# Threshold attention into a gMLP block: new order of the gate branch, the weight preparation, the first clears and the last products

## The chip, the cores and the metric

One core of a Trainium2 chip runs the whole kernel. The metric is device time in microseconds (us), the median of several executions. The core's engines run side by side, each in its own program order: TensorE (PE; weight loads are listed as PEld), VectorE (DVE), ScalarE (ACT), GpSimd (POOL) and SyncE (SP). DMA transfers are issued from an engine's queue (SPq, POOLq, ACTq), also in order.

## The reference

```python
scores = scale * np.matmul(q, k.transpose(0, 1, 3, 2))          # 8 batches, 8 heads, 576 x 576
thresh = np.max(scores, axis=-1, keepdims=True) - tau
scores = np.where(scores >= thresh, scores, -1000000000.0)
attn = np.exp(scores - np.max(scores, axis=-1, keepdims=True))
attn = attn / (np.sum(attn, axis=-1, keepdims=True) + 1e-09)
x = (attn @ v), heads side by side                              # 8 x 576 x 512
h = np.maximum(x @ w_in, 0.0); u, v = halves of h               # 512 columns each
v_n = (v - mean) / np.sqrt(var + 1e-06)                         # over the 512 columns
v_s = np.einsum('ts,bsd->btd', w_spatial, v_n) + b_spatial[None, :, None]
out = (u * v_s) @ w_out                                         # float32
```

## The kernel before

Two heads make a pair; 32 pairs, four to a batch. A pair takes five **steps** (`g = 5 * slot + c`), one per block of 128 query rows (the fifth has 64). In a step TensorE forms the scores of both heads (L426, L429, into one of two `ps_s` buffers), VectorE takes the negated row maximum (`negm`, L472), ScalarE the exponential (`e`, L480), and one step later VectorE sets the values under the threshold to zero (`p`, L445; `pr`, L454, in the last block). SP then transposes the masked rows by DMA (`pT`, L449, once for two blocks; `ptr`, L457). So the 160 `negm` rows of VectorE mark the 160 steps; step 0 is the first.

Beside the scores each step carries up to two jobs, `f1` (before the maximum) and `f2` (at the step's end). In blocks 0 to 2 one of them prepares the next pair (transposes of q and k, L221 and L234); in blocks 3 and 4 one is `pv`, the product with v for the pair before (L261), whose result `xn` SP transposes into `xT` (L275). The other is a gMLP job of an earlier batch. There are 20 per batch:

- `moe_v` (five): half v of `x @ w_in` (L289), `vrel` on ScalarE (L314); one or two steps later a square with its sum (`sq`, L322), then a chain on GpSimd that ends in the normalised rows `vn` (L328).
- `moe_u` (five): half u, transposed (L340, L345).
- `moe_s` (five): the spatial product (L370, L375), each over all five `vn` blocks, and the gate `gT` on VectorE (L384).
- `moe_o` (five): the product with `w_out` (L399), a copy, a store (L410).

From step 27 on (`LAG`) batch b's jobs start at step 27 + 20b: v and u alternate over ten steps, then s and o alternate (o of the batch before). An `act` job used as `f2` is evaluated at the start of the next step (`held`). Each job takes one of two `ps_f` banks. The loads of q, k and v are popped from `queue`, one a step, ahead of the step's own work. A dictionary `chores` places the weight preparation: `w_in` at steps 5 to 11, `w_spatial` at 12 to 14, its casts and transposes at 16 to 20, the bias at 2 and 21, `w_out` at 23 and 25. After the last scores `last` lists the remaining jobs, two a step.

All clears of padding stand at the head of GpSimd's program. SP has one queue for loads, transposes and stores.

Of the kernel before, what the change touches and what calls it, by code (L numbers as in the profile page):

```python
# [17 lines left out]
def kernel(  # L18
# [49 lines left out]
    p_ring = [const.tile([P, 2, 1152], BF16, name=f"p{i}") for i in range(2)]
    pr_ring = [const.tile([P, 640], BF16, name=f"pr{i}") for i in range(2)]
# [4 lines left out]
    for ts in ld_ring:  # L74
        for t in ts:
            nc.gpsimd.memset(t[64:128, :, 4, :], 0.0)
    vx_ring = [const.tile([P, 2, D], F32, name=f"vx{i}") for i in range(2)]
    for t in vx_ring:
        nc.gpsimd.memset(t[0:64], 0.0)
    kd_ring = [const.tile([P, P], F32, name=f"kd{i}") for i in range(2)]  # L80
    for t in kd_ring:
        nc.gpsimd.memset(t, 0.0)
    for t in v_ring:
        nc.gpsimd.memset(t[:, :, D:D + 1], 1.0)
        nc.gpsimd.memset(t[64:128, 4, D:D + 1], 0.0)
        nc.gpsimd.memset(t[64:128, 9, D:D + 1], 0.0)
        nc.gpsimd.memset(t[0:64, 10, D:D + 1], 0.0)
    ptr_ring = [const.tile([P, 5, 192], BF16, name=f"ptr{i}") for i in range(3)]
    for t in ptr_ring:
        nc.gpsimd.memset(t[:, :, 128:192], 1.0)  # L90
    for t in pr_ring:
        nc.gpsimd.memset(t[:, S:640], 0.0)
    for t in vn_ring:
        nc.gpsimd.memset(t[64:128, 4, :], 1.0)

    w_in = const.tile([P, 4, 1024], BF16, name="w_in")
    w_o = const.tile([P, 4, 512], BF16, name="w_o")
# [1 line left out]
    wsb = const.tile([P, 5, 640], BF16, name="wsb")  # L99


    def load(i, n, w):

        b, hp = divmod(i, HP)
        t = ld_ring[i // 2 % 2][w][:, 2 * (i % 2):2 * (i % 2) + 2 * n]
        src = (q, k, v)[w][b, 2 * hp:2 * hp + 2 * n]

        def main():
            nc.sync.dma_start(
                out=t[:, :, 0:4, :],  # L110
                in_=src[:, 0:512, :].rearrange("h (p c) d -> p h (c d)", c=4))

        def rest():
            nc.sync.dma_start(out=t[0:64, :, 4, :],
                              in_=src[:, 512:576, :].rearrange("h p d -> p h d"))
# [130 lines left out]
    def pv(i, h):  # L246
        b, hp = divmod(i, HP)
        hold = {}
        vt = v_ring[i % 4]

        def mm():
            t = hold["t"] = bank()
            for c in range(5):
                for j in range(5):
                    if c < 4:
                        lhs = pts[i, c // 2][:, c % 2, 4 + (j + 1) % 5 if h else j, :]
                        rhs = vt[:, (10 if j == 4 else 5 + j) if h else j, :]
                    else:
                        lhs = pts[i, 2][:, j, 64 * h:64 * h + P]
                        rhs = vt[:, 5 * h + j, :]  # L260
                    nc.tensor.matmul(out=t[:, c * 65:c * 65 + 65], lhsT=lhs, rhs=rhs,  # L261
                                     start=(j == 0), stop=(j == 4))

        def ev():
            o = hold["t"][:, 0:325].rearrange("p (c d) -> p c d", d=65)
            if h == 0:
                xns[i] = xp.tile([P, 5, P], BF16, name="xn")
            r = small.tile([P, 5], F32, name="r")
            nc.vector.reciprocal(out=r, in_=o[:, :, 64])
            nc.vector.tensor_tensor(out=xns[i][:, :, h * D:(h + 1) * D], in0=o[:, :, 0:64],  # L270
                                    in1=r.unsqueeze(2).broadcast_to([P, 5, 64]), op=ALU.mult)
            if h == 1:
                if hp == 0:
                    xts[b] = xtp.tile([P, 4, 640], BF16, name="xT")
                nc.sync.dma_start_transpose(  # L275
                    out=xts[b][:, hp, :].rearrange("p (c s) -> p c s", s=P),
                    in_=xns[i].rearrange("p c d -> p (c d)"))
        return "dve", mm, ev

    us, gs = {}, {}  # L280
    later = []

    def moe_v(b, c):
        hold = {}

        def mm():
            t = hold["t"] = bank()
            for f in range(4):
# [103 lines left out]
    def moe_o(b, c):  # L392
        hold = {}
        n = P if c < 4 else 64

        def mm():
            t = hold["t"] = bank()
            for f in range(4):
                nc.tensor.matmul(out=t[:n], lhsT=gs[b][:, f, c * P:c * P + n],  # L399
                                 rhs=w_o[:, f, :], start=(f == 0), stop=(f == 3))  # L400

        def ev():
            o = orr.tile([P, 512], F32, name="o")
# [6 lines left out]
            nc.sync.dma_start(out=dst, in_=o[:n])  # L410
        return "act", mm, ev


# [45 lines left out]
    def step(i, c, f1, f2):  # L459

        if i is not None:
            s = scores(i, c)
# [14 lines left out]
        if i is not None:  # L477
            e = ep.tile([P, 2, S], F32, name="e")
            for h in range(nh):
                nc.scalar.activation(out=e[:, h, :], in_=s[:, h, :], func=ACT.Exp,  # L480
                                     bias=nm[:, h:h + 1])
        if unmasked:
            mask()
        if i is not None:
            unmasked.append((i, c, e))
        for f in due:
# [6 lines left out]
                held.append(f2[2])  # L493


    chores = {2: (load_bias, 0)}
    for n, g0, d, f in ((4, 5, 2, load_w_in), (3, 12, 1, load_ws), (5, 16, 1, shape_ws),
                        (1, 21, 1, shape_bias), (2, 23, 2, load_w_o)):
        chores.update({g0 + d * j: (f, j) for j in range(n)})

    LAG = 27
    jobs = {}
    for b in range(B - 1):
        for j in range(5):
            g = LAG + 20 * b + 2 * j
            jobs[g], jobs[g + 1] = (moe_v, b, j), (moe_u, b, j)
            jobs[g + 10] = (moe_s, b, j)
            if b:  # L510
                jobs[g + 11] = (moe_o, b - 1, j)
    last = [jobs.pop(g) for g in range(5 * NPAIR, LAG + 20 * B) if g in jobs]
    last += [(moe_o, B - 2, j) for j in range(5)]
    last[6:6] = [(pv, NPAIR - 1, h) for h in range(2)]
    last += [(f, B - 1, j) for f in (moe_v, moe_u, moe_s, moe_o) for j in range(5)]
    with tc.manual_schedule():
        for w in (0, 1):
            for f in load(0, 1, w):
                f()
        shape_qk(0)  # L520
        for f in (qk_main(0, 0), qk_main(0, 1), qk_rem(0)):
            f[1]()
            f[2]()
        for w in (0, 1):
            for f in load(1, 1, w):
                f()
        shape_qk(1)
        for f in load(0, 2, 2):
            f()
        queue = []  # L530
        for g in range(5 * NPAIR + (len(last) + 1) // 2):
            slot, c = divmod(g, 5)
# [64 lines left out]
```

## Time and profile before

| | us |
|---|---|
| median of 3 runs (581.0 to 581.65) | 581.09 |
| the profiled execution | 579.05 |
| its span, first to last instruction | 577.3 |
| mean granted TensorE clock | 0.94 |

The profile is of one execution; 1.75 us of its time lie outside the span. A row of a timeline has start, duration, engine, line, operation, tiles, and in brackets the idle time of the engine before it with what ended it. A count xN on a row means that neighbours were merged.

### The profile page before, as it was taken

What the parts mean: (1) busy time and instruction counts of PE and PEld (TensorE: products, weight loads), DVE (VectorE), ACT (ScalarE), POOL (GpSimd) and SP (SyncE); (2) the same over time, 40 slices, a digit from 0 to 9 for tenths busy, and PEclk for the clock granted to TensorE, in tenths of its full rate; (3) what the DMA queues carried; (4) which work ended last, traced back from release to release, by engine and by line L of the source; (5) the groups of instructions that cost most, each with busy time, mean ns of one, the idle gap of its engine ahead of it and who ended that gap; (6) DMA issues with size and microseconds to landing.
All of it is one profiled execution on the core that took longest, in us unless ns stands there. A gap on an engine that the chain in (4) does not pass through costs nothing.

```text
span 577.3 us, 10207 instructions
## 1 busy us (share of the span) xinstructions
PE 489.6 (85%) x3796; PEld 258.5 (45%) x3840; DVE 464.7 (81%) x512; ACT 329.3 (57%) x609; POOL 235.2 (41%) x436
## 2 busy tenths in 40 slices
PE   3785765996989699996999889996999969998896
PEld 2443333553545355553545445552555535553442
DVE  0897984995999779996999969995899959997543
ACT  1554451784557635784567835784557736685261
POOL 7532880275206612275206622276025722054010
PEclk9997985997999989998999989998999979998999
DMA  7599998978487876978698765977679677654732
GB/s 215 99 199 186 211 177 141 218 127 198 88 174 161 175 136 151 194 151 161 144 190 193 164 157 140 193 152 177 145 150 218 142 163 149 126 105 86 157 103 82
DMA packets 243601, 90.91 MB, mean 157 GB/s; under 512 B 213024, under 2 KB 238112, under 8 KB 243552
## 3 DMA queue, kind: packets, MB, share of 16 engines
q1 hardware_dynamic: 242352, 88.68, 73.9%
q0 software_dynamic: 1200, 1.58, 2.0%
q8 instruction: 30, 0.49, 0.3%
q14 instruction: 19, 0.16, 0.1%
HBM read 33.31 MB, written 9.44 MB: 74 GB/s over the span
## 4 chain that ended last, share of the span: by engine, by line
PE 47%; DVE 22%; issue 8%; POOL 7%; ACT 7%; DMA 7%; SPq 2%; POOLq 0%; ACTq 0%; DVEq 0%
PE s L426 18%; DVE negm L472 9%; DVE p L445 9%; PE f L261 7%; PE f L289 6%; PE s L429 4%; ACT e L480 3%; PE f L340 3%; PE f L370 3%; PE f L399 3%; DMA pT<-p 2%; PE f L221 2%; ACT sq L322 2%; DVE gT L384 1%; DMA ptr<-pr 1%
## 5 line engine op out<-in xcount | busy, mean ns | idle before, releaser
L480 ACT ACTIVATE e<-s,negm 128x576 f32<-128x576 f32 x288 | 199.6, 739 | 104.3 <-DVE negm L472 89.4
L472 DVE TENSOR_REDUCE negm<-s 128x2 f32<-128x1152 f32 (+1 forms) x160 | 197.1, 1232 | 45.8 <-PE s L426 44.3
L426 PE MATMUL s<-qkT 64*128 64x512 f32 (+1 forms) x768 | 194.3, 598 | 1.0 <-ACT e L480 1.0
L445 DVE SCALAR_TENSOR_TENSOR p<-e,ctau 128x1152 bf16<-128x1152 f32 x128 | 186.8, 1459 | 3.5 <-DMA pT<-p 3.5
L242 POOL COPY kd<-qkT 64x64 f32<-64x64 f32 x32 | 14.1, 442 | 168.2 <-ACT qkT L238 168.1
L261 PEld LDWEIGHTS <-pT 128*128 128x128 bf16 x1280 | 50.4, 101 | 43.9 <-issue 19.4
L426 PEld LDWEIGHTS s<-qkT 64*128 64x128 f32 (+1 forms) x768 | 56.7, 176 | 29.7 <-issue 3.7
L225 ACT COPY qkT<-f 128x512 f32<-128x512 f32 x64 | 37.6, 588 | 50.8 <-PE f L221 50.8
L429 PE MATMUL s<-kd,qkT 128*128 128x128 f32 x256 | 57.2, 307 | 10.9 <-ACT e L480 9.8
L261 PE MATMUL f<-v,pT 128*128 128x65 bf16 x1260 | 54.1, 199 | 14.2 <-DMA pT<-p 11.3
L370 PE MATMUL f<-wsT,vn 128*128 128x512 bf16 x130 | 38.5, 389 | 31.6 <-POOL vn L328 28.7
L429 PEld LDWEIGHTS s<-kd,qkT 128*128 128x128 f32 x256 | 46.3, 202 | 25.8 <-ACT e L480 11.5
L407 ACT COPY o<-f 128x512 f32<-128x512 f32 (+1 forms) x32 | 18.7, 583 | 53.8 <-PE f L399 51.8
L289 PE MATMUL f<-w_in,xT 128*128 128x512 bf16 x142 | 37.9, 380 | 5.5 <-ACT uT L355 5.1
L384 DVE TENSOR_TENSOR gT<-f,uT 128x512 bf16<-128x512 f32 x30 | 20.6, 686 | 25.9 <-PE f L370 22.2
L140 POOL COPY kn<-kl 128x640 f32<-128x640 f32 x32 | 31.1, 972 | 24.4 <-DMA kl<-in_k_dram 21.0
L370 PEld LDWEIGHTS <-vn 128*128 128x128 bf16 x160 | 14.8, 97 | 50.9 <-POOL vn L328 32.1
L316 POOL TENSOR_SCALAR nmean<-sm 128x1 f32<-128x1 f32 x35 | 15.7, 448 | 52.6 <-ACT vrel L314 52.6
L399 PE MATMUL f<-w_o,gT 128*128 128x512 bf16 (+1 forms) x126 | 36.5, 413 | 0.3 <-issue 0.2
L270 DVE TENSOR_TENSOR xn<-f,r 128x320 bf16<-128x320 f32 x63 | 31.0, 492 | 2.2
L328 POOL TENSOR_SCALAR vn<-vrel,rs,nm 128x512 bf16<-128x512 f32 (+1 forms) x35 | 30.4, 867 | 3.8
L340 PE MATMUL f<-xT,w_in 128*128 128x512 bf16 x104 | 29.9, 380 | 0.8
(92 smaller groups left out, 524.7 us busy)
## 6 DMA issues: line engine op xcount, KB each, us to landing
vl<-in_v_dram SPq DMA_DIRECT2D x16, 512.0 KB, 4.3
out_dram<-o SPq DMA_DIRECT2D x32, 256.0 KB, 2.5
ql<-in_q_dram SPq DMA_DIRECT2D x15, 512.0 KB, 4.3
kl<-in_k_dram SPq DMA_DIRECT2D x15, 512.0 KB, 5.1
uT<-in_moe_w_spatial_dram SPq DMA_DIRECT2D x2, 576.0 KB, 5.3
vl<-in_v_dram SPq DMA_DIRECT2D x16, 64.0 KB, 2.7
pT<-p SPq DMA_TRANSPOSE x64, 5.3
w_in<-in_moe_w_in_dram POOLq DMA_DIRECT2D x4, 256.0 KB, 5.6
```

The costliest lines, as they stand in the source:

```text
L140: nc.gpsimd.tensor_copy(out=t, in_=src)
L225: nc.scalar.copy(out=qks[i][:, which, 0:512], in_=hold["t"])
L261: nc.tensor.matmul(out=t[:, c * 65:c * 65 + 65], lhsT=lhs, rhs=rhs, start=(j == 0), stop=(j == 4))
L289: nc.tensor.matmul(out=t, lhsT=xts[b][:, f, c * P:(c + 1) * P], rhs=w_in[:, f, 512:1024], start=(f == 0), stop=(f == 3))
L340: nc.tensor.matmul(out=t, lhsT=w_in[:, m, f * P:(f + 1) * P], rhs=xts[b][:, m, 0:512], start=(m == 0), stop=(m == 3))
L370: nc.tensor.matmul(out=t, lhsT=vn[:, c, f * P:(f + 1) * P], rhs=wsT[:, c, 0:512], start=(c == 0), stop=(c == 4))
L399: nc.tensor.matmul(out=t[:n], lhsT=gs[b][:, f, c * P:c * P + n], rhs=w_o[:, f, :], start=(f == 0), stop=(f == 3))
L426: return nc.tensor.matmul(out=out, lhsT=qk[hs, 0, m], rhs=qk[hs, 1, lo:lo + n], start=True, stop=True)
L429: nc.tensor.matmul(out=view(s, 512, [[448, 2], [1, 64]]), lhsT=qk[:, 0, c * P:(c + 1) * P], rhs=kd_ring[i % 2], start=True, stop=True)
L445: nc.vector.scalar_tensor_tensor(out=pt[:, c % 2, :], in0=ef, scalar=ctau, in1=ef, op0=ALU.is_ge, op1=ALU.mult)
L472: nc.vector.tensor_reduce(out=nm[:, 0:nh], in_=s, axis=AX.X, op=ALU.max, negate=True)
L480: nc.scalar.activation(out=e[:, h, :], in_=s[:, h, :], func=ACT.Exp, bias=nm[:, h:h + 1])
```

## The change

It has six parts.

1. The order of a batch's jobs becomes `vuvvuvuvuu` then `oososososs`: all v by position 7, the first s at position 12 (it was 10, behind v at 8), the last at 19.
2. `chores` is spread: `w_in` at 6, 10, 14, 18; `w_spatial` at 8, 12, 16; the bias at 13, 15, and its three placing DMAs apart at 37; casts and transposes at 23, 26, 29, 32, 35; `w_out` at 42 and 47.
3. `sends`: the `xT` transposes and the stores are no longer issued where they arise but after the next mask, behind its `pT` or `ptr`.
4. The clears: three stay ahead of the first shaping; the others come behind pair 0's preparation, the bf16 ones on VectorE.
5. The first k load is issued from ScalarE's queue, the loads of pair 1 and v come earlier, and eight transposes of the identity run on TensorE first.
6. The tail: the last batch's v products run over the first three parts of the sum (`moe_v_part`) while the fourth `xT` is on its way, then over the fourth; the `moe_o` jobs of the batch before are dealt around them.

```diff
+    def clear_first():
+        for t in ld_ring[0][:2]:
             nc.gpsimd.memset(t[64:128, :, 4, :], 0.0)
+        nc.gpsimd.memset(kd_ring[0], 0.0)
+    def clear_rest():
+        ...
+        for t in ptr_ring:
+            nc.vector.memset(t[:, :, 128:192], 1.0)
...
-                nc.sync.dma_start_transpose(
+                xn = xns[i]
+                sends.append(lambda: nc.sync.dma_start_transpose(
...
+    def moe_v_part(b, c):
+        def mm():
+            if c % 3 == 0:
+                parted["tile"] = ps_s.tile([P, 1536], F32, name="s")
+            t = parted[c] = parted["tile"][:, 512 * (c % 3):512 * (c % 3) + 512]
+            for f in range(3):
+                nc.tensor.matmul(out=t, lhsT=xts[b][:, f, c * P:(c + 1) * P],
+                                 rhs=w_in[:, f, 512:1024], start=(f == 0), stop=False)
...
+        ready = sends[:]
+        sends.clear()
         if unmasked:
             mask()
+        for f in ready:
+            f()
...
-    chores = {2: (load_bias, 0)}
+    chores = {13: (load_bias, 0)}
...
+    ORDER = "vuvvuvuvuu" + "oososososs"
...
+    last += [(moe_o, Z - 1, j) for j in (0, 1)]
+    last += [(pv, NPAIR - 1, h) for h in range(2)]
+    last += [(moe_v_part, Z, j) for j in range(5)]
+    last += [(moe_v, Z, j) for j in range(5)]
+    last += [(moe_o, Z - 1, j) for j in (2, 3, 4)]
+    last += [(f, Z, j) for f in (moe_u, moe_s, moe_o) for j in range(5)]
...
-            for f in load(0, 1, w):
+            for f in load(0, 1, w, (nc.sync, nc.scalar)[w]):
                 f()
+        clear_first()
...
+        for _ in range(8):
+            nc.tensor.transpose(out=ps_f.tile([P, 512], F32, name="f")[:, 0:P], in_=identf,
+                                identity=identf)
```

TensorE before, behind batch 1's last u product (L345, step 56): scores (L429, L426), the remainder's transposes (L234), then the first spatial product.

```order
L345 LDWEIGHTS w_in
L345 MATMUL f<-xT,w_in 128x64
L429 MATMUL s<-kd_135,qkT 128x2x64
L426 MATMUL s<-qkT 128x512 x2
L234 MATMUL f<-identf,qn 128x128
L234 MATMUL f<-identf,kn 128x128
L370 LDWEIGHTS vn_117
L370 MATMUL f<-wsT,vn_117 128x512
```

The same place of the changed kernel, whose lines have other numbers (L364 is the last u product, L418 the product with `w_out`).

```order
L364 LDWEIGHTS w_in
L364 MATMUL f<-xT,w_in 128x64
L448 MATMUL s<-kd_120,qkT 128x2x64
L445 MATMUL s<-qkT 128x512 x2
L239 MATMUL f<-identf,qn 128x128
L239 MATMUL f<-identf,kn 128x128
L418 LDWEIGHTS gT
L418 MATMUL f<-w_o,gT 128x512
```

Where the spatial product stood there is now a product of the batch before; the spatial one follows two steps later.

SP's queue before, around the fourth `xT` of a batch (steps 63 to 65; `ql_118` is the next load of q).

```order
L449 DMA_TRANSPOSE pT<-p_108 128x18x128
L410 DMA out_dram<-o 128x512 x2
L449 DMA_TRANSPOSE pT<-p_109 128x18x128
L275 DMA_TRANSPOSE xT<-xn 128x5x128
L109 DMA ql_118<-in_q_dram 128x4x256
L457 DMA_TRANSPOSE ptr_154<-pr_110 128x5x128
L114 DMA ql_118<-in_q_dram 64x4x64
```

The same stretch of the changed kernel (L281 is `xT`, L476 is `ptr`, L429 a store).

```order
L468 DMA_TRANSPOSE pT<-p_101 128x18x128
L429 DMA out_dram<-o 128x512
L468 DMA_TRANSPOSE pT<-p_102 128x18x128
L429 DMA out_dram<-o 64x512
L111 DMA ql_111<-in_q_dram 128x4x256
L476 DMA_TRANSPOSE ptr_121<-pr_103 128x5x128
L281 DMA_TRANSPOSE xT<-xn 128x5x128
```

The fourth `xT` has moved behind the load of q and behind `ptr`.

GpSimd before, at the first shaping (`qn`, `kn`); 28 more clears and the identity stand ahead of these rows.

```order
L90 MEMSET ptr_156 128x5x64
L92 MEMSET pr_110 128x64
L92 MEMSET pr_111 128x64
L94 MEMSET vn_116 64x512
L94 MEMSET vn_117 64x512
L137 TENSOR_SCALAR qn<-ql_118 128x640
L140 COPY kn<-kl_119 128x640
```

The changed kernel's GpSimd from its first clear on.

```order
L76 MEMSET ql_111 64x4x64
L76 MEMSET kl_112 64x4x64
L77 MEMSET kd_119 128x128
masks.py:197 MEMSET identf 128x128
masks.py:199 ISA
masks.py:199 AFFINE_SELECT identf<-identf 128x128
L139 TENSOR_SCALAR qn<-ql_111 128x640
L142 COPY kn<-kl_112 128x640
```

Three clears and the identity are left ahead of `qn`.

## Rows read from the trace of the kernel before

**Rows 1.** The page's busy time by engine.

```profile
PE 489.6 (85%) x3796; PEld 258.5 (45%) x3840; DVE 464.7 (81%) x512; ACT 329.3 (57%) x609; POOL 235.2 (41%) x436
```

**Rows 2.** Who waited for whom: total us, times, longest.

```profile
PE f L370 <- POOL vn L328: 28.7, 7, 4.4
```

**Rows 3.** Timeline of TensorE around batch 2's first spatial product.

```profile
263.34 1.02 PE L370 MATMUL f<-wsT,vn 128*128 128x512 bf16 x3
...
268.75 0.39 PE L370 MATMUL f<-wsT,vn 128*128 128x512 bf16 x1 [4.38 <-POOL vn L328]
...
269.36 2.08 PE L426 MATMUL s<-qkT 64*128 64x512 f32 x4
...
277.02 1.13 PE L426 MATMUL s<-qkT 64*128 64x512 f32 x4
```

**Rows 4.** Timeline of ScalarE and GpSimd in the same stretch.

```profile
265.76 0.72 ACT L322 ACTIVATE sq<-vrel,nmean 128x512 bf16<-128x512 f32 x1
...
267.93 0.76 POOL L328 TENSOR_SCALAR vn<-vrel,rs,nm 64x512 bf16<-64x512 f32 x1
```

**Rows 5.** Timeline of VectorE: maxima of steps 0, 11, 26, 72, 74, 77, 78, 79, 98.

```profile
14.44 1.36 DVE L472 TENSOR_REDUCE negm<-s 128x2 f32<-128x1152 f32 x1 [13.55 <-PE s L426]
...
43.71 1.35 DVE L472 TENSOR_REDUCE negm<-s 128x2 f32<-128x1152 f32 x1
...
101.33 1.35 DVE L472 TENSOR_REDUCE negm<-s 128x2 f32<-128x1152 f32 x1
...
248.82 1.36 DVE L472 TENSOR_REDUCE negm<-s 128x2 f32<-128x1152 f32 x1 [0.94 <-PE s L426]
...
254.66 0.75 DVE L472 TENSOR_REDUCE negm<-s 128x1 f32<-128x576 f32 x1
...
263.06 1.34 DVE L472 TENSOR_REDUCE negm<-s 128x2 f32<-128x1152 f32 x1
...
271.49 1.36 DVE L472 TENSOR_REDUCE negm<-s 128x2 f32<-128x1152 f32 x1 [1.62 <-PE s L426]
...
274.95 0.76 DVE L472 TENSOR_REDUCE negm<-s 128x1 f32<-128x576 f32 x1
...
337.37 1.36 DVE L472 TENSOR_REDUCE negm<-s 128x2 f32<-128x1152 f32 x1 [1.75 <-PE s L426]
```

**Rows 6.** Stretches of 10 us: busy PE, PEld, DVE, ACT, POOL, clock, DMA, GB/s.

```profile
40.00:50.00 10.00, 6.82 (x40) 3.20 (x38) 6.87 (x7) 4.76 (x8) 1.44 (x1) 1.00 1.27 154
...
300.00:310.00 10.00, 9.89 (x91) 5.63 (x93) 9.70 (x12) 6.88 (x14) 3.02 (x8) 1.00 0.91 222
```

**Rows 7.** Timeline of SP's queue and TensorE at batch 3's first v product.

```profile
296.12 1.24 SPq L275 DMA_TRANSPOSE xT<-xn  x1
...
298.30 1.57 SPq L457 DMA_TRANSPOSE ptr<-pr  x1
...
299.60 1.23 PE L289 MATMUL f<-w_in,xT 128*128 128x512 bf16 x3
```

**Rows 8.** DMA issues: count, KB each, median us from issue to landing.

```profile
kl<-in_k_dram SPq DMA_DIRECT2D x2, 32.0 KB, 3.1
...
xT<-xn SPq DMA_TRANSPOSE x32, 2.6
```

**Rows 9.** Timeline of the first 13 us.

```profile
2.67 0.63 SPq L114 DMA_DIRECT2D kl<-in_k_dram  x1
...
7.39 0.73 POOL L137 TENSOR_SCALAR qn<-ql 128x640 f32<-128x640 f32 x1
...
12.31 2.08 PE L426 MATMUL s<-qkT 64*128 64x512 f32 x4
```

**Rows 10.** Timeline of TensorE before step 24.

```profile
90.37 0.73 PE L261 MATMUL f<-v,pT 128*128 128x65 bf16 x10 [7.22 <-DMA pT<-p]
```

**Rows 11.** Timeline of the tail: the last transpose and the first v product.

```profile
547.27 1.21 SPq L275 DMA_TRANSPOSE xT<-xn  x1
...
553.17 1.04 PE L289 MATMUL s<-w_in,xT 128*128 128x512 bf16 x4
```

More of the change, by code (lines that the diff above doesn't have):

```diff
@@ L73 @@
                for i in range(2)]
-    for ts in ld_ring:
-        for t in ts:
-            nc.gpsimd.memset(t[64:128, :, 4, :], 0.0)
[L77 to L94, printed above, removed]
+    vx_ring = [const.tile([P, 2, D], F32, name=f"vx{i}") for i in range(2)]
+    kd_ring = [const.tile([P, P], F32, name=f"kd{i}") for i in range(2)]
+    ptr_ring = [const.tile([P, 5, 192], BF16, name=f"ptr{i}") for i in range(3)]
+    def clear_first():
+        for t in ld_ring[0][:2]:
+            nc.gpsimd.memset(t[64:128, :, 4, :], 0.0)
+        nc.gpsimd.memset(kd_ring[0], 0.0)
+    def clear_rest():
+        nc.gpsimd.memset(ld_ring[0][2][64:128, :, 4, :], 0.0)
+        nc.gpsimd.memset(kd_ring[1], 0.0)
+        for t in vx_ring:
+            nc.gpsimd.memset(t[0:64], 0.0)
+        for t in ld_ring[1]:
+            nc.gpsimd.memset(t[64:128, :, 4, :], 0.0)
+        for t in v_ring:
+            nc.vector.memset(t[:, :, D:D + 1], 1.0)
+            nc.vector.memset(t[64:128, 4, D:D + 1], 0.0)
+            nc.vector.memset(t[64:128, 9, D:D + 1], 0.0)
+            nc.vector.memset(t[0:64, 10, D:D + 1], 0.0)
+        for t in ptr_ring:
+            nc.vector.memset(t[:, :, 128:192], 1.0)
+        for t in pr_ring:
+            nc.vector.memset(t[:, S:640], 0.0)
+        for t in vn_ring:
+            nc.vector.memset(t[64:128, 4, :], 1.0)
     w_in = const.tile([P, 4, 1024], BF16, name="w_in")
@@ L99, with load @@
     wsb = const.tile([P, 5, 640], BF16, name="wsb")
-    def load(i, n, w):
+    def load(i, n, w, eng=nc.sync):
         b, hp = divmod(i, HP)
@@ L108, in main @@
         def main():
-            nc.sync.dma_start(
+            eng.dma_start(
                 out=t[:, :, 0:4, :],
@@ L113, in rest @@
         def rest():
-            nc.sync.dma_start(out=t[0:64, :, 4, :],
-                              in_=src[:, 512:576, :].rearrange("h p d -> p h d"))
+            eng.dma_start(out=t[0:64, :, 4, :],
+                          in_=src[:, 512:576, :].rearrange("h p d -> p h d"))
         def rest_b():
@@ L196, in shape_bias, with place_bias @@
         nc.gpsimd.tensor_copy(out=parts[:, 2, :], in_=b32)
+    def place_bias(_):
         for n in range(3):
@@ L210 @@
     done_with = set()
+    sends = []
     qks, pts, xns, xts = {}, {}, {}, {}
@@ L274, in ev @@
                     xts[b] = xtp.tile([P, 4, 640], BF16, name="xT")
-                nc.sync.dma_start_transpose(
+                xn = xns[i]
+                sends.append(lambda: nc.sync.dma_start_transpose(
                     out=xts[b][:, hp, :].rearrange("p (c s) -> p c s", s=P),
-                    in_=xns[i].rearrange("p c d -> p (c d)"))
+                    in_=xn.rearrange("p c d -> p (c d)")))
         return "dve", mm, ev
@@ L281 @@
     later = []
+    parted = {}
+    def moe_v_part(b, c):
[6 more added lines that the diff above has]
+                                 rhs=w_in[:, f, 512:1024], start=(f == 0), stop=False)
+        return "act", mm, lambda: None
     def moe_v(b, c):
@@ L286, in mm @@
         def mm():
-            t = hold["t"] = bank()
-            for f in range(4):
+            t = hold["t"] = parted.get(c) if b == B - 1 else bank()
+            for f in range(3 if b == B - 1 else 0, 4):
                 nc.tensor.matmul(out=t, lhsT=xts[b][:, f, c * P:(c + 1) * P],
@@ L409, in ev @@
                    else out[b, 512:576, :])
-            nc.sync.dma_start(out=dst, in_=o[:n])
+            sends.append(lambda: nc.sync.dma_start(out=dst, in_=o[:n]))
         return "act", mm, ev
@@ L493, in step @@
                 held.append(f2[2])
-    chores = {2: (load_bias, 0)}
-    for n, g0, d, f in ((4, 5, 2, load_w_in), (3, 12, 1, load_ws), (5, 16, 1, shape_ws),
-                        (1, 21, 1, shape_bias), (2, 23, 2, load_w_o)):
+    chores = {13: (load_bias, 0)}
+    for n, g0, d, f in ((4, 6, 4, load_w_in), (3, 8, 4, load_ws), (5, 23, 3, shape_ws),
+                        (1, 15, 1, shape_bias), (1, 37, 1, place_bias), (2, 42, 5, load_w_o)):
         chores.update({g0 + d * j: (f, j) for j in range(n)})
@@ L503 @@
     LAG = 27
+    ORDER = "vuvvuvuvuu" + "oososososs"
     jobs = {}
     for b in range(B - 1):
[L506 to L511, printed above, removed]
-    last = [jobs.pop(g) for g in range(5 * NPAIR, LAG + 20 * B) if g in jobs]
-    last += [(moe_o, B - 2, j) for j in range(5)]
-    last[6:6] = [(pv, NPAIR - 1, h) for h in range(2)]
@@ L515 @@
-    last += [(f, B - 1, j) for f in (moe_v, moe_u, moe_s, moe_o) for j in range(5)]
+        n = dict.fromkeys("vuso", 0)
+        for j, t in enumerate(ORDER):
+            f = {"v": moe_v, "u": moe_u, "s": moe_s, "o": moe_o}[t]
+            if t != "o" or b:
+                jobs[LAG + 20 * b + j] = (f, b - (t == "o"), n[t])
+            n[t] += 1
+    last = [jobs.pop(g) for g in range(5 * NPAIR, LAG + 20 * B) if g in jobs]
+    Z = B - 1
+    last += [(moe_o, Z - 1, j) for j in (0, 1)]
+    last += [(pv, NPAIR - 1, h) for h in range(2)]
@@ L516 @@
+    last += [(moe_v_part, Z, j) for j in range(5)]
+    last += [(moe_v, Z, j) for j in range(5)]
+    last += [(moe_o, Z - 1, j) for j in (2, 3, 4)]
+    last += [(f, Z, j) for f in (moe_u, moe_s, moe_o) for j in range(5)]
     with tc.manual_schedule():
         for w in (0, 1):
-            for f in load(0, 1, w):
+            for f in load(0, 1, w, (nc.sync, nc.scalar)[w]):
                 f()
+        clear_first()
+        make_identity(nc, identf)
+        nc.vector.memset(ntau, -float(tau))
+        nc.vector.memset(mhalf, -0.5)
+        nc.scalar.activation(out=ctau, in_=ntau, func=ACT.Exp)
+        for w in (0, 1):
+            for f in load(1, 1, w):
+                f()
+        for f in load(0, 2, 2):
+            f()
+        for _ in range(8):
+            nc.tensor.transpose(out=ps_f.tile([P, 512], F32, name="f")[:, 0:P], in_=identf,
+                                identity=identf)
@@ L523 @@
             f[2]()
-        for w in (0, 1):
-            for f in load(1, 1, w):
-                f()
+        clear_rest()
         shape_qk(1)
-        for f in load(0, 2, 2):
-            f()
         queue = []
@@ L561 @@
             held.pop(0)()
+        for f in sends:
+            f()
 _INS = ['q', 'k', 'v', 'tau', 'moe_w_in', 'moe_w_spatial', 'moe_b_spatial', 'moe_w_out']
```

4 lines of the change are left out of this document (removed).

## The prediction

> **What bounds the kernel now.** I read the page's busy times first. TensorE is busy for 85% of the span, VectorE for 81% [rows 1]: both near full, so an average names no bound and the stages have to be read apart. The maxima of VectorE give the stages, one row a step [rows 5]. Steps 0 to 11 take 43.71 - 14.44 = 29.27 us, 2.66 us a step, with no gMLP jobs in them. Steps 11 to 26 take 101.33 - 43.71 = 57.6 us, where fifteen such steps would take 39.9: 17.7 us too much. From step 27 on the pattern repeats every 20 steps; steps 78 to 98 take 337.37 - 271.49 = 65.9 us. In such a stretch 10 us without a stall show TensorE busy for 9.89 and VectorE for 9.70 [rows 6], so what is left to gain there is the stalls.
>
> The list of waits names the stall: TensorE waits for `vn` seven times, 28.7 us in all [rows 2], once per batch that has scores beside it. The timeline shows one: three of the five matmuls of the first spatial product run at 263.34, the last starts at 268.75 behind an idle of 4.38 us, and the scores behind it take 2.08 us for four where they take 1.13 later [rows 3]. TensorE thus ran at about half its later speed after the wait, its 1.2 GHz level against 2.4, though only the row's duration shows that so sharply. What it waited for is the last block's square on ScalarE at 265.76 and the GpSimd chain that ends with `vn` at 267.93 [rows 4]. The fifth v product stands two steps ahead of the first spatial product and its square one step later, in the same step in which TensorE already stands at the product.
>
> **The change part by part.** *Job order (the main term).* The step pair with the stall, 77 and 78, takes 274.95 - 263.06 = 11.89 us. The pair 72 and 73 holds the same blocks (2 and 3) with two ordinary jobs and takes 254.66 - 248.82 = 5.84 us [rows 5]. One stall so costs 6.05 us: 4.38 of waiting and 1.67 of slow matmuls. Scaled to all seven waits that is 28.7 x 6.05 / 4.38 = 39.6 us. In the changed order the last v is at position 7 and in block 4, where its `vrel` is taken in the same step; its square falls into position 8, and the spatial product stands at 12. Three to four steps of about 3 us lie between, against a chain of 268.75 - 265.76 = 3 us. The wait goes, and no matmul is added: the same 20 jobs stand in the 20 steps. Bounds: at least the bare 28.7 us if the slow matmuls were hidden by VectorE anyway, at most 43 us (six pairs like this one and the last batch). I take 39.6, since the step difference is measured whole. What is late next is TensorE itself: 65.9 - 6.05 = 59.8 us for 20 steps of which it is busy nearly throughout.
>
> *The later `xT`.* A new wait: SP now issues the fourth `xT` of a batch behind the load of q and behind `ptr`. In the rows `xT` was issued at 296.12 and lands a median 2.6 us after issue, at 298.7, and the first v product began at 299.60, 0.9 us later [rows 7, 8]. The fourth matmul, which needs that part, comes some 0.65 us behind the first (three of 1.23 us, overlapping). With the two instructions exchanged, `ptr` goes out at about 297.0 and `xT` behind its 1.57 us, at 298.6, landing at 301.2; TensorE wants it at 300.3. That is 0.9 us, less the bit by which the wait before it fills; I take 0.8 us x 7 batches = 5.6 us lost. Behind the waiting product stand the next step's scores, for which VectorE then waits. Bounds: nothing, if the steps ahead are longer; 7 x (0.9 + 1.67) = 18 us, if each wait also costs a slow stretch like the one above. Its nearest rows are waits under 1 us, so I stay near the lower part. The stores deferred with it cost nothing: they are behind `pT` instead of ahead, and three `o` buffers cover them.
>
> *Chores.* Steps 11 to 26 lose 17.7 us. DMA is more than full at 40 to 50 us (busy share 1.27) [rows 6], and before step 24 TensorE waits 7.22 us for a `pT` [rows 10] that stands in SP's queue behind transposes of the spatial weights, which wait for GpSimd's casts. The change takes four of five of those transposes, the placing of the bias and both loads of `w_out` out of these steps, and starts two of four `w_in` loads later. All `w_in` and `w_spatial` bytes still fall within steps 6 to 18. I leave 5 us of the 17.7, so 13 gained; bounds 3 (only the later half of one stall) and 17.7. What was moved to steps 27 to 47 lies beside jobs on a TensorE that is nearly full, and GpSimd, at 41%, has room; I charge 1 us, from 0 to 5. The loads of `w_out` are due at step 57, the bias at 39; neither is near.
>
> *Start.* `qn` starts at 7.39, when GpSimd's list of clears ends; the last k load was issued at 2.67 and lands a median 3.1 us later, at 5.8 [rows 8, 9]. Three clears and the identity end well before that. With k issued beside q, from about 1.3, everything lands by 4.4 to 5, and step 0 starts 2.5 to 3 us earlier. The clears moved behind it (about 2 us on GpSimd) lie where TensorE makes pair 0's scores; the ones on VectorE lie in the 13.55 us it waits [rows 5]. I take 3.4 us with the second pair's loads, which no longer wait behind pair 0; bounds 0.5 (only DMA order) and 6. The eight extra transposes end before the data are there and I cost them at nothing. The first scores run slow at 12.31 (2.08 us) although ten transposes had run just ahead [rows 9]. The Trainium skill (TensorE: Matmul & The Clock Gate, Part 4: PE-mode transpose) says that transposes do not count as busy for the clock; by that the eight gain nothing, otherwise the sum would be about 2 us lower. The Trainium skill (DMA: Bandwidth & Descriptors, Issuing engines are not separate DMA queues) says that issuing from a second engine saves only the time to initiate; by that the k load gains no more than the issue rows of q, and the start term would be nearer 2.
>
> *Tail.* The last `xT` is issued at 547.27, lands at about 549.9, and the v products start at 553.17 behind six jobs put there to fill the wait [rows 8, 11]. In the new order 15 of the 20 v matmuls fill it and only five follow. Part of them still runs slow after the wait for `ptr`, so I place the first complete v product at 551.6, some 2.6 us before its old end, 554.2. From there VectorE sets the pace, five statistics and five normalisations, and it keeps the lead. `ptr` is issued 0.6 us later, since `xT` goes ahead of it. Gain 2.0; bounds -1 (a loss) and 5.
>
> **The sum**, against the profiled 579.05 us: -39.6 + 5.6 - 13 + 1 - 3.4 - 2.0 = -51.4, which gives 527.65. The median of the runs lies 2.04 above the profiled execution, so 529.7 us.
>
> **Rivals.**
> - *The start stays bound by DMA.* For: all w_in and w_spatial traffic still falls into steps 6 to 18, at a share already over 1 [rows 6]. Against: the 7.22 us wait comes of the weight transposes, which are moved. Then 3 instead of 13: 540 us. Chance 0.17.
> - *`xT` and TensorE take more back.* TensorE is the bound between the stalls [rows 6], and a late `xT` hits it there. With 2 us a batch instead of 0.8 the time is 538. Chance 0.13.
> - *The stall only moves: the change doesn't do what it says.* GpSimd works in order, and casts of weights or loads awaited ahead of the `vn` chain could keep `vn` last for position 12. Half the main term lost: 549.5. Against it: four steps of margin to a 3 us chain. Chance 0.05.
> - *Slower: the SP queue becomes the bound.* Without the stall SP has 60 us instead of 66 for the same DMAs, and the fourth `xT` stands at the end of its queue. If it landed 7.6 us after issue (5 more than the median) in all seven batches, each wait would be 0.8 + 5 + 1.67 = 7.5 us, 52 instead of 5.6, and if the same crowding kept the 13 us of the chores, the time is 529.7 + 46.7 + 13 = 589. It decides from a wait of some 6.3 us per batch on. Against: only a few `xT` are late now; the v products wait for one hardly at all [rows 7]. Chance 0.05, of which 0.01 within the bound of no change.
> - *All parts work in full:* no late `xT`, all 17.7 us of the chores back, 3 us more at both ends: 516. Chance 0.08.
>
> **How the numbers follow.** The forecast, 529.7, has 0.52, with a range of its own of 520 to 538. To hold 8 in 10 the range takes in the case above it (540), the low bounds of the start and tail, and much of the 538 case with both together: 516 to 546. Left out are the moved stall, the slower case and the best case's lower half, about 0.14. A difference under 0.2% (1.2 us) could not be told from none. Faster 0.95, same 0.01, slower 0.04.
>
> **What would show it.** In the changed profile the wait of the spatial product for `vn` should be gone, the step with position 10 should take about 2.8 us and 20 steps about 60.5; the v product should wait for `xT` under 1 us per batch; step 0's maximum should stand at 11, step 26's near 85; the last v should end near 553. The forecast is wrong if 20 steps still take over 62 us, or step 26 comes after 95.

## The result and the profile after

The changed kernel takes 564.6 us (median; 562.84 to 566.71) against 581.05 before: ratio 0.973, 95% interval 0.968 to 0.978. It is faster, but 35 us slower than forecast and outside the range. The profiled execution took 562.84 us, its span is 561.1. Ratios here and below are of executions in the chip's usual state; in the run "xT at once" two of four were in a slower one, the profiled one among them.

The busy time by engine answers to [rows 1]: TensorE does the same work in a shorter span.

```profile
PE 487.0 (87%) x3848; PEld 257.7 (46%) x3848; DVE 470.5 (84%) x535; ACT 328.2 (59%) x609; POOL 240.8 (43%) x413
```

In the list of waits of the changed kernel (total us, times, longest) nothing stands for `vn` and the spatial product any more: the row of [rows 2] is gone. The waits of `pv` for `ptr` have grown (6.0 us in four waits before). New are those of the v product (L308) for `xT`, and two for a bank that ScalarE still reads (`vrel`). The wait for `uT` is now one of the u product (it was 5.1 us, of the v product).

```profile
PE f L266 <- DMA ptr<-pr: 19.2, 10, 6.1
...
PE f L308 <- DMA xT<-xn: 9.5, 5, 3.4
...
PE f L359 <- ACT vrel L333: 5.8, 7, 0.8
...
PE f L266 <- ACT vrel L333: 4.6, 7, 0.7
PE f L364 <- ACT uT L374: 4.5, 6, 0.8
```

The maxima of VectorE (L491 now) at steps 0, 11, 26, 57, 77, 97, 157 and 159 answer to [rows 5].

```profile
12.47 1.36 DVE L491 TENSOR_REDUCE negm<-s 128x2 f32<-128x1152 f32 x1 [8.13 <-PE s L445]
...
41.67 1.35 DVE L491 TENSOR_REDUCE negm<-s 128x2 f32<-128x1152 f32 x1
...
93.81 1.35 DVE L491 TENSOR_REDUCE negm<-s 128x2 f32<-128x1152 f32 x1
...
193.22 1.36 DVE L491 TENSOR_REDUCE negm<-s 128x2 f32<-128x1152 f32 x1 [0.63 <-PE s L445]
...
256.27 1.36 DVE L491 TENSOR_REDUCE negm<-s 128x2 f32<-128x1152 f32 x1 [0.63 <-PE s L445]
...
323.31 1.36 DVE L491 TENSOR_REDUCE negm<-s 128x2 f32<-128x1152 f32 x1 [0.63 <-PE s L445]
...
512.67 1.34 DVE L491 TENSOR_REDUCE negm<-s 128x2 f32<-128x1152 f32 x1
...
518.64 0.75 DVE L491 TENSOR_REDUCE negm<-s 128x1 f32<-128x576 f32 x1
```

Steps 57 to 77 take 256.27 - 193.22 = 63.1 us, 77 to 97 67.0, where 60.5 was forecast and more than 62 was to show the forecast wrong. The differences of such rows give the stages, with the best experiment on the cause (nothing deferred, below) in the last column:

| profiled span, us | before | changed | nothing deferred |
|---|---|---|---|
| to step 0 | 14.4 | 12.5 | 12.3 |
| steps 0 to 11 | 29.3 | 29.2 | 29.6 |
| steps 11 to 26 | 57.6 | 52.1 | 47.4 |
| steps 26 to 57 | 95.3 | 99.4 | 99.7 |
| steps 57 to 157 | 329.0 | 319.5 | 303.7 |
| steps 157 to 159 | 9.3 | 6.0 | 6.0 |
| behind step 159 | 42.4 | 42.5 | 39.3 |

How a batch's first v product goes in the changed kernel answers to [rows 7]. First SP's queue: the load of q, `ptr`, then the fourth `xT`.

```profile
284.69 0.55 SPq L111 DMA_DIRECT2D ql<-in_q_dram  x1
285.34 1.24 SPq L476 DMA_TRANSPOSE ptr<-pr  x1
286.63 2.85 SPq L281 DMA_TRANSPOSE xT<-xn  x1
```

Then TensorE: three of four matmuls, 3.36 us of idle, the fourth, and scores that take 1.61 us instead of 1.13.

```profile
288.03 0.81 PE L308 MATMUL f<-w_in,xT 128*128 128x512 bf16 x3 [0.22 <-DVE gT L406]
292.19 0.39 PE L308 MATMUL f<-w_in,xT 128*128 128x512 bf16 x1 [3.36 <-DMA xT<-xn]
...
292.73 1.61 PE L445 MATMUL s<-qkT 64*128 64x512 f32 x4
```

The granted clock was 1.00 from 280 to 288 us; behind the wait it was 0.61, for the most part the lower of TensorE's two levels (1.2 GHz; full speed is 2.4). In the answer below it is the third number from the end, ahead of the DMA share.

```profile
292.50:296.00 3.50, 3.50 (x12) 1.03 (x11) 1.62 (x2) 0.69 (x2) 0.19 (x1) 0.61 1.11 284
```

From issue to the matmul are 292.19 - 286.63 = 5.6 us; [rows 8] had a median of 2.6 for the landing. Four of the five transposes that TensorE waited for stood behind a load of q that was still under way; they landed 3.6 to 5.5 us after issue. Over all `xT` of the changed kernel (minimum, median, maximum):

```profile
DMA to landing us min/median/max: 2.6/3.4/5.5
```

### The profile page after: what moved, and what is told of

It is laid out like the page before. It is cut to its first block, busy times and chain, and to the rows that moved or that the text cites. A ratio compares the mean times of both kernels' runs of the same rounds, so it can differ in the third digit from the quotient of the medians.

```text
span 561.1 us, 10240 instructions
## 1 busy us (share of the span) xinstructions
PE 487.0 (87%) x3848; PEld 257.7 (46%) x3848; DVE 470.5 (84%) x535; ACT 328.2 (59%) x609; POOL 240.8 (43%) x413
## 4 chain that ended last, share of the span: by engine, by line
PE 47%; DVE 24%; DMA 12%; ACT 10%; issue 5%; SPq 1%; POOL 0%; ACTq 0%; POOLq 0%
PE s L445 18%; DVE negm L491 14%; PE f L266 7%; DVE p L464 7%; DMA ptr<-pr 7%; ACT e L499 5%; PE f L389 4%; DMA xT<-xn 4%; PE s L448 3%; PE f L359 3%; PE f L308 3%; PE f L418 3%; ACT sq L341 2%; DVE xn L275 1%; ACT vrel L333 1%
## 5 line engine op out<-in xcount | busy, mean ns | idle before, releaser
L491 DVE TENSOR_REDUCE negm<-s 128x2 f32<-128x1152 f32 (+1 forms) x160 | 197.2, 1233 | 47.3 <-PE s L445 45.9
L445 PE MATMUL s<-qkT 64*128 64x512 f32 (+1 forms) x768 | 191.1, 590 | 1.0 <-ACT e L499 1.0
L445 PEld LDWEIGHTS s<-qkT 64*128 64x128 f32 (+1 forms) x768 | 55.6, 173 | 29.2 <-issue 2.8
L448 PE MATMUL s<-kd,qkT 128*128 128x128 f32 x256 | 55.4, 299 | 8.5 <-ACT e L499 5.5
L308 PE MATMUL f<-w_in,xT 128*128 128x512 bf16 x140 | 37.8, 387 | 11.0 <-DMA xT<-xn 9.5
L142 POOL COPY kn<-kl 128x640 f32<-128x640 f32 x32 | 26.1, 817 | 32.8 <-DMA kl<-in_k_dram 20.3
L335 POOL TENSOR_SCALAR nmean<-sm 128x1 f32<-128x1 f32 x35 | 11.8, 338 | 64.8 <-ACT vrel L333 64.8
L266 PE MATMUL f<-v,ptr 128*128 128x65 bf16 x315 | 21.2, 199 | 19.2 <-DMA ptr<-pr 19.2
L359 PE MATMUL f<-xT,w_in 128*128 128x512 bf16 x120 | 32.6, 396 | 5.8 <-ACT vrel L333 5.8
L139 POOL TENSOR_SCALAR qn<-ql 128x640 f32<-128x640 f32 x32 | 30.5, 953 | 11.6 <-DMA ql<-in_q_dram 10.7
L418 PE MATMUL f<-w_o,gT 128*128 128x512 bf16 (+1 forms) x128 | 33.8, 388 | 0.5
L333 ACT ACTIVATE vrel<-f 128x512 f32<-128x512 f32 x35 | 20.8, 595 | 20.8 <-PE f L308 20.8
L473 DVE SCALAR_TENSOR_TENSOR pr<-e,ctau 128x576 bf16<-128x576 f32 x32 | 31.9, 997 | 0.0
```

Of the source, the lines that this page charges most:

```text
L359: nc.tensor.matmul(out=t, lhsT=w_in[:, m, f * P:(f + 1) * P], rhs=xts[b][:, m, 0:512], start=(m == 0), stop=(m == 3))
L445: return nc.tensor.matmul(out=out, lhsT=qk[hs, 0, m], rhs=qk[hs, 1, lo:lo + n], start=True, stop=True)
L448: nc.tensor.matmul(out=view(s, 512, [[448, 2], [1, 64]]), lhsT=qk[:, 0, c * P:(c + 1) * P], rhs=kd_ring[i % 2], start=True, stop=True)
L491: nc.vector.tensor_reduce(out=nm[:, 0:nh], in_=s, axis=AX.X, op=ALU.max, negate=True)
```

## The experiments

Each run is compared with the kernel before, run on the same chip in the same call; ratios carry their 95% interval. The changed kernel's is 0.973.

**xT at once.** The deferral is undone for `xT` alone:

```diff
-                sends.append(lambda: nc.sync.dma_start_transpose(
+                nc.sync.dma_start_transpose(
```

> The changed kernel, but xT is issued on SP where xn arises, as before; the stores stay deferred. Theory Q (order in SP's queue): the fourth xT of a batch lands late because it stands behind the 512-KB load of q and ptr; issued first, the five waits of TensorE for it (9.5 us) and the slow matmuls behind them (some 2 us) go: about 553 where the changed kernel has 564.6. Rival D (the DMA engines are full once the vn stall is gone): what xT gains ptr and pT lose, within 2 us of 564.6.

Ratio 0.936 (0.928 to 0.944). The rival is out: `ptr` loses nothing that `xT` gains (TensorE's waits for it are 12.9 us, against 19.2 in the changed kernel). More came back than the 11 us expected.

**Only the job order**, in the kernel before:

```diff
+    ORDER = "vuvvuvuvuu" + "oososososs"
...
-            jobs[g], jobs[g + 1] = (moe_v, b, j), (moe_u, b, j)
-            jobs[g + 10] = (moe_s, b, j)
...
+                jobs[LAG + 20 * b + j] = (f, b - (t == "o"), n[t])
```

> The kernel before with the new job order alone (xT and stores at once, weight preparation, clears and tail as before). Theory Q: the vn stall goes and nothing is put behind loads, so the whole main term shows: 581 - 40 = 541, 20 steps in about 60 us. Rival D: without the stall the transposes land late all the same, 20 steps take 63 to 65 us as in the changed kernel: 560 to 568.

548.2 us, ratio 0.945 (0.939 to 0.950). So the order alone is worth 580.3 - 548.2 = 32.1 us, more than all six parts together, and the rival (20 steps in 63 to 65 us) is out: they take 60.9, as the maxima of steps 57 and 77 show.

```profile
194.12 1.36 DVE L472 TENSOR_REDUCE negm<-s 128x2 f32<-128x1152 f32 x1 [0.63 <-PE s L426]
...
255.05 1.36 DVE L472 TENSOR_REDUCE negm<-s 128x2 f32<-128x1152 f32 x1 [0.63 <-PE s L426]
```

**The old job order** in the changed kernel:

```diff
-    ORDER = "vuvvuvuvuu" + "oososososs"
+    ORDER = "vuvuvuvuvu" + "sososososo"
```

> The changed kernel with the job order of before; all else changed. Theory Q: the seven waits for vn come back (about 40 us with slow matmuls), and in their slack the waits for xT (9.5 us plus 2) go: 564.6 + 40 - 11 = about 593. Rival D (the transposes had always needed that time, the stall only hid it): the stall costs what the lateness costs, 564 to 572.

592.4 us, ratio 1.020 (1.013 to 1.027): the other parts of the change, without the order, make the kernel slower. The maxima of steps 77 and 97 in this run are 69.4 us apart, 3.9 more than before the change. The stall for `vn` does not hide the late transposes as Theory Q had it: both waits stand in the list, and both are paid, though the total came out as that theory said.

```profile
263.04 1.34 DVE L491 TENSOR_REDUCE negm<-s 128x2 f32<-128x1152 f32 x1
...
332.42 1.34 DVE L491 TENSOR_REDUCE negm<-s 128x2 f32<-128x1152 f32 x1
```

```profile
PE f L389 <- POOL vn L347: 24.3, 6, 4.4
...
PE f L308 <- DMA xT<-xn: 10.1, 6, 2.5
```

**Nothing deferred**: `xT` and the stores at once.

```diff
-            sends.append(lambda: nc.sync.dma_start(out=dst, in_=o[:n]))
+            nc.sync.dma_start(out=dst, in_=o[:n])
```

> The changed kernel with xT and stores both issued at once. Theory Q: as with xT alone at once, and the tail gains about 1.5 us more, since the last xT no longer waits for five stores and the copies for their buffers: about 551.5. Rival D: within 2 us of 564.6. If the stores at once block SP ahead of pT, slower than with xT alone.

543.0 us, ratio 0.936 (0.929 to 0.942): not to be told from `xT` alone. The deferral cost 564.6 - 543.0 = 21.6 us. The maxima of steps 26, 57, 77, 97 and 157 show where: 20 steps take 60.9 us from step 57 on (59.9 the last time).

```profile
89.25 1.35 DVE L490 TENSOR_REDUCE negm<-s 128x2 f32<-128x1152 f32 x1
...
188.91 1.36 DVE L490 TENSOR_REDUCE negm<-s 128x2 f32<-128x1152 f32 x1 [0.63 <-PE s L444]
...
249.86 1.36 DVE L490 TENSOR_REDUCE negm<-s 128x2 f32<-128x1152 f32 x1 [0.63 <-PE s L444]
...
310.80 1.36 DVE L490 TENSOR_REDUCE negm<-s 128x2 f32<-128x1152 f32 x1 [0.63 <-PE s L444]
...
492.64 1.34 DVE L490 TENSOR_REDUCE negm<-s 128x2 f32<-128x1152 f32 x1
```

**The load behind xT**: deferral kept, but the loads popped behind the step, so SP's order is `ptr`, `xT`, load of q.

```diff
+            step(i, c, fs[0] if fs else None, fs[1] if len(fs) > 1 else None)
             for f in queue[:1 if g > 4 else 2]:
                 queue.pop(0)()
-            step(i, c, fs[0] if fs else None, fs[1] if len(fs) > 1 else None)
```

> The changed kernel with the deferral kept, but each load of q, k and v is issued behind the step's transposes instead of ahead of them, so that xT stands behind ptr and ahead of the 512-KB load of q. In the changed kernel xT took 5.6 us from issue (286.63) to the matmul that waited (292.19), where its median before was 2.6. Theory L (the load's packets stand before xT in the DMA engines): xT lands some 2.6 us after issue again, the waits for it fall under 0.5 us, 20 steps take 61 us: 545 to 550. Rival P (what counts is the place behind ptr, a step later): xT still lands behind the v product, 20 steps 63 to 66 us: 558 to 565.

549.9 us, ratio 0.946 (0.941 to 0.950). The row of waits for `xT` falls from 9.5 us to 1.6, and the median landing from 3.4 us to 2.7:

```profile
PE f L308 <- DMA xT<-xn: 1.6, 5, 0.5
```

```profile
DMA to landing us min/median/max: 2.6/2.7/5.5
```

So the lateness is above all the 512-KB load ahead of `xT`, not the place behind `ptr`. Some 7 us still lack to 543.0. This run's list has 20.4 us of waits for `ptr`, against 9.4 with nothing deferred; why `ptr` is late here was not tested.

**The old weight preparation**, nothing deferred.

```diff
-    chores = {13: (load_bias, 0)}
...
+    chores = {2: (load_bias, 0)}
+    for n, g0, d, f in ((4, 5, 2, load_w_in), (3, 12, 1, load_ws), (5, 16, 1, shape_ws),
+                        (1, 21, 1, shape_bias), (2, 23, 2, load_w_o)):
```

> Nothing deferred (543.0) and the weight preparation at the steps of before. Theory H (spreading only moves the loss: what steps 11 to 26 gain, some 10 us, steps 26 to 57 lose): within 4 us of 543, so 541 to 547. Rival G (spreading is worth most of the 13 us that were forecast): 552 to 556.

543.4 us, ratio 0.934 (0.931 to 0.938). By the medians spreading is worth nothing: steps 11 to 26 take 52.0 us instead of 47.4, steps 26 to 57 94.4 instead of 99.7. (Steps 0 to 11 take 33.1 instead of 29.6, and the two profiled executions lie 4.2 us apart; the executions of nothing deferred spread over 6.)

**Casts early**, nothing deferred: the casts of the spatial weights at steps 17 to 22, their transposes left at 23 to 35.

```diff
+    def send_ws(c):
         nc.sync.dma_start_transpose(out=wsT[:, :, c * P:(c + 1) * P], in_=wsb[:, c, :])
...
+    chores.update({g: (shape_ws, j) for j, g in enumerate((17, 19, 20, 21, 22))})
```

> Nothing deferred, and the casts of the spatial weights moved to steps 17, 19, 20, 21, 22, while their DMA transposes stay at 23, 26, 29, 32, 35. Theory H1 (in steps 26 to 57 SP's queue stands still at a weight transpose that waits for a cast, which waits in GpSimd's order behind the vn chain; ptr behind it is late, 3.5 us and slow matmuls): steps 26 to 57 take 94 us instead of 99.7, about 537. Rival D1 (the DMA work itself is the load on these steps): 541 to 544.

539.6 us, ratio 0.928 (0.922 to 0.934; the interval overlaps that of nothing deferred). Steps 26 to 57 take 95.9 us, near the 94 expected. But that stage differs as much between runs that are alike in it: it took 99.7 us with nothing deferred and 97.5 in two tiles in turn (below), both with the late casts, and 98.0 in casts early and two tiles. What the edit was meant to mend is seen in the run with nothing deferred: on GpSimd the fifth cast ends at 122.7, behind a chain of `vn` and casts of v; SP, whose turn the weight transpose is, issues it only then, `ptr` behind it, and TensorE waits 3.5 us for `ptr`.

```profile
121.33 1.36 POOL L188 CAST wsb<-gT 64x64 bf16<-64x64 f32 x1
```

```profile
122.72 1.20 SPq L189 DMA_TRANSPOSE wsT<-wsb  x1
123.97 0.58 SPq L111 DMA_DIRECT2D ql<-in_q_dram  x1
124.65 2.18 SPq L475 DMA_TRANSPOSE ptr<-pr  x1
```

```profile
129.06 0.33 PE L266 MATMUL f<-v,ptr 128*128 128x65 bf16 x5 [3.50 <-DMA ptr<-pr]
```

With the casts early `ptr` goes out 3.3 us behind the `xT` ahead of it (at 119.80) instead of 5.2, but TensorE still waits 2.47 us for it:

```profile
123.10 1.22 SPq L477 DMA_TRANSPOSE ptr<-pr  x1
...
128.81 0.33 PE L268 MATMUL f<-v,ptr 128*128 128x65 bf16 x5 [2.47 <-DMA ptr<-pr]
```

So the standing queue is shown, but it explains about 1 us of that wait. What the edit is worth in all is not clear of the spread between runs, and the rival (the DMA work itself) is not out.

**Two tiles in turn** for the last v products, nothing deferred.

```diff
-            t = parted[c] = parted["tile"][:, 512 * (c % 3):512 * (c % 3) + 512]
...
+            t = parted[c] = parted["tile", c % 2][:, 512 * (c // 2):512 * (c // 2) + 512]
```

> Nothing deferred, and the last batch's v products dealt over the two PSUM tiles in turn (0, 2, 4 in one, 1, 3 in the other) instead of three and two in a row. Theory T (a product into a tile waits until ScalarE has read its neighbour in the same tile: 2.4 us in three waits): most of 2.4 us gone on the way to the first statistics, VectorE's chain sets the rest: 541 to 542.5 where 543 was. Rival V (the statistics on VectorE end last anyway): 543 within 0.5.

539.4 us, ratio 0.929 (0.925 to 0.934). The rows show 1.2 us of it: behind the maximum of step 159 the span has 38.1 us instead of 39.3. TensorE now stands at the first spatial product before the last `vn` is there (0.23 us of idle), so VectorE's chain ends last from then on. The rest of the difference between the medians is within the spread between runs.

```profile
523.29 1.03 PE L388 MATMUL f<-wsT,vn 128*128 128x512 bf16 x3
...
524.56 0.39 PE L388 MATMUL f<-wsT,vn 128*128 128x512 bf16 x1 [0.23 <-DVE vn L327]
```

**Casts early and two tiles** together, and **loads spread** further on top of that.

```diff
-    for n, g0, d, f in ((4, 6, 4, load_w_in), (3, 8, 4, load_ws), (5, 23, 3, send_ws),
...
+    for n, g0, d, f in ((4, 6, 6, load_w_in), (3, 9, 6, load_ws), (5, 26, 2, send_ws),
+                        (1, 16, 1, shape_bias), (1, 36, 1, place_bias), (2, 33, 2, load_w_o)):
...
```

> Nothing deferred, casts early and last v products over two tiles in turn: the two edits that each gave about 3.5 us together. If both are real: 539.6 - 1.2 (what the tail rows of the second alone show) = 538.4, at best 536. If the two medians were the spread between runs of the same kernel: 540 to 543.

> Nothing deferred, casts early, last v products over two tiles in turn, and the weight loads spread further: w_in at 6, 12, 18, 24, w_spatial at 9, 15, 21, the weight transposes at 26 to 34, w_out at 33 and 35, the bias at 36. Theory W (steps 11 to 26 still lose 8 us because too many loads fall into steps 6 to 18, and wider spacing lets ptr land in time): 531 to 535. Rival D2 (DMA is full from step 6 to 40 in any order, the loss only moves): as e11, 537 to 540.

Together 537.6 us, ratio 0.928 (0.924 to 0.932); spread further 544.2, ratio 0.937 (0.933 to 0.942). Theory W falls: nothing is gained, and steps 11 to 57 take 148.4 us instead of 146.5. That DMA is simply full there, wherever the loads stand, is likely, but not shown by itself.

**v and u in turn**, with both of these edits.

```diff
-    ORDER = "vuvvuvuvuu" + "oososososs"
+    ORDER = "vuvuvuvuvu" + "oososososs"
```

> As the version with casts early and two tiles (537.6), but v and u alternate again over the first ten positions; the s and o positions stay those of the change. Theory B (20 steps take 60.9 instead of the forecast 59.8 because after two v in a row a product waits for a bank that ScalarE still reads: 5.8 and 4.6 us over seven batches, 1.5 us a batch): those waits go, the older wait for uT (0.7 us a batch) may come back: 20 steps in 60.0 to 60.4, 532 to 535. Rival N (the last v, now at position 8, is late for the first s at 12, or the bank waits only move): 536 to 541; if vn is late, a wait for vn is in the trace.

534.1 us, ratio 0.922 (0.918 to 0.925), the best version found, 30 us under the changed kernel. Its interval just meets that of the version without the edit, but steps 57 to 157 take 300.7 us instead of 303.6: 20 steps take 60.1 to 60.5, the last time 59.3. Both `vrel` rows are gone from its list of waits, and the v product waits for `uT` as in the kernel before, as Theory B allowed; new are 2.4 us of `pv` behind a copy of `o`. In all 7.5 us of waits for a bank stand where 14.9 stood. So the banks are part of what 20 steps take over the forecast, not all of it; the spatial product waits for no `vn` of these batches.

```profile
PE f L309 <- ACT uT L375: 5.1, 7, 0.7
```

## Why the prediction was wrong

- **What bounds the kernel: right.** The `vn` wait was the largest stall, and removing it was worth more than the whole change.
- **The job order, -39.6 us: right in mechanism, too large.** Alone it gave 32.1. The two steps that lost the stall behave as worked out (positions 10 and 11: 256.27 to 262.26, 5.99 us for the forecast 5.84). The "59.8 us for 20 steps" is what failed: they take 60.9. In part that is because v products that stand one behind the other make the next product wait for a bank, and u products likewise (5.8, 4.6 and 4.5 us over seven batches in the rows above); I counted jobs and matmuls and left out the banks. With v and u in turn 20 steps take 60.1 to 60.5; the rest stays open.
- **The later `xT`, +5.6 us: the step that failed.** The text took "`xT` ... lands a median 2.6 us after issue" from rows in which `xT` stood ahead of the load of q, and kept that figure for a place behind a 512-KB load. There the transposes took 3.6 to 5.5 us. The issue itself came as forecast: 1.4 us ahead of the first v product (288.03 - 286.63), where 1.0 was worked out. (The one `xT` read in [rows 7] had itself landed after 4.3 us, by the trace, and not at 298.7.) The waits for `xT` are 9.5 us over five batches; waits for `ptr` and slow matmuls come on top, so that steps 57 to 157 lose 319.5 - 303.7 = 15.8 us. The text's upper bound for them, 18 us, held that; its choice of a value near the lower end did not. With 4.7 us in steps 11 to 26 and 3.2 in the tail, where the text looked for next to none, the deferral costs 21.6 us by the medians.
- **The chores, -13 + 1 us: failed.** With nothing else in the way the spreading gives 0.4 us. Steps 11 to 26 gain, and 26 to 57 lose as much: part of that is that the casts queue behind the `vn` chain on GpSimd and hold SP's queue, the rest is open. The text priced GpSimd by its mean (41%) and SP not at all. It had also put the wrong cause to the 7.22 us of [rows 10]: in the kernel before, GpSimd's last cast of the spatial weights ended at 71.60, 11 us ahead of the issue of the `pT` that TensorE waited for, which then took 7.7 us to land.

```profile
71.37 0.23 POOL L186 CAST wsb<-gT 64x64 bf16<-64x64 f32 x1
```

```profile
82.61 3.88 SPq L449 DMA_TRANSPOSE pT<-p  x1
```

  Within the changed kernel `ptr` also came late behind step 13; what delayed it was not tested:

```profile
55.14 0.46 PE L266 MATMUL f<-v,ptr 128*128 128x65 bf16 x5 [6.11 <-DMA ptr<-pr]
```

- **The start, -3.4 us: right, too large.** Step 0 came 1.97 us earlier, as much as `qn` did (5.42 instead of 7.39). What holds `qn` now is not the clears but the load of q, which lands later than the "4.4 to 5" of the text; `kn` follows without a wait, so the k load did not set the start. The first scores still ran slow.

```profile
5.42 0.72 POOL L139 TENSOR_SCALAR qn<-ql 128x640 f32<-128x640 f32 x1 [3.35 <-DMA ql<-in_q_dram]
```

```profile
2.12 2.29 PE L559 MATMUL f<-identf 128*128 128x128 f32 x8 [2.12 <-POOL identf masks.py:199]
...
10.34 2.08 PE L445 MATMUL s<-qkT 64*128 64x512 f32 x4
```

  The Trainium skill (TensorE: Matmul & The Clock Gate, Part 4: PE-mode transpose) says that transposes do not count as busy for the clock. The rows agree in so far as the eight transposes of the identity gained nothing that shows. They ended at 4.4, well before the first scores at 10.34, so the run does not tell whether transposes as such or the pause decides.
- **The tail, -2.0 us: nothing came in the changed kernel, 3.1 us without the deferral.** The third `xT` of the last batch, now deferred, goes out between `pT` and `ptr`; `ptr` and the five stores behind it go out later by its time. The copy of `o` at 530.03 follows 4.47 us of idle, the partial products wait 1.72 us for such a copy, and the last `xT`, ready behind `xn` at 530.74, goes out at 532.10, behind the five stores:

```profile
523.97 1.73 SPq L281 DMA_TRANSPOSE xT<-xn  x1
...
527.13 4.88 SPq L429 DMA_DIRECT2D out_dram<-o  x5
...
530.03 0.59 ACT L426 COPY o<-f 128x512 f32<-128x512 f32 x1 [4.47 <-PE s L266]
...
531.70 3.40 PE L298 MATMUL s<-w_in,xT 128*128 128x512 bf16 x15 [1.72 <-ACT o L426]
...
532.10 1.29 SPq L281 DMA_TRANSPOSE xT<-xn  x1
...
536.00 0.38 PE L308 MATMUL s<-w_in,xT 128*128 128x512 bf16 x1 [0.69 <-ACT vrel L318]
```

  The stores alone do not cost this. In the run "xT at once" they are still deferred, five of them still stand ahead of the last `xT`, and the span behind step 159 is 39.3 us, as with nothing deferred; its partial products start without a wait. So "the stores deferred with it cost nothing" holds as far as these two profiles tell, and the loss is the deferred `xT`'s.

```profile
519.80 3.40 PE L297 MATMUL s<-w_in,xT 128*128 128x512 bf16 x15
...
520.57 1.24 SPq L280 DMA_TRANSPOSE xT<-xn  x1
```

  The row at 536.00 above is the other thing I had not seen: in this program a product into a tile waits until ScalarE has read its neighbour in that tile. The sign "the last v should end near 553" was on the clock of the kernel before, later than the forecast's own end, and could show nothing (it ended at 539.05).

The measured terms add up: -32 for the order, +22 for the deferral, 0 for the chores, -2 and -3 at the ends make -15, where -16.5 was measured. Of the 35 us between forecast and result the later `xT` is some 16, the chores 12 and the order 7.5. The rival "`xT` and TensorE take more back" had the wait right (2 us a batch; 9.5 / 5 = 1.9 measured), and "the start stays bound by DMA" had its direction. "The SP queue becomes the bound" had the mechanism, the `xT` at the end of its queue, but with a landing of 7.6 us that no batch reached. I gave each a time of its own and a range that held one or two of them. They share SP's queue and came together.

## What to carry to other kernels

A transfer's time to landing belongs to its place in the queue: when a small transpose is moved behind a large load, take the landing of the rows that stand behind such loads, not its own median. Before deferring an issue, ask for each one moved who waits for it next; here the one transpose with a near reader cost two thirds of what the removed stall had given. Test the parts of a change singly: the best part alone beat the whole, and one line undone gave 21.6 us back.

## What the runs showed of the hardware

A DMA transpose of 128 x 640 bf16 landed 2.6 us after issue with no other transfer under way (the kernel before, the last `xT` at 547.27), and 3.6 to 5.5 us after issue behind a 512-KB load of q of the same queue (the changed kernel, four batches). With the load issued behind them instead the waits for these transposes fell from 9.5 to 1.6 us.

An idle of 3.36 us on TensorE was followed by scores at 1.61 us and a u product at 1.89 us for four matmuls (1.13 and 1.04 otherwise), at a granted clock of 0.61. I had priced the slow stretch at 1.67 us for an idle of 4.38.
